# A two-layer linear-attention and gated-MLP kernel: new engine assignments, new order numbers, and a shorter assumed transfer time

## The chip, the cores and the metric

The kernel runs on one core of one Trainium2 chip. The core has engines with instruction queues of their own: TensorE (PE, matrix products), VectorE (DVE), ScalarE (ACT), GpSimd (POOL) and SyncE (SP, which here only starts transfers). Each queue is worked off in order; semaphores hold an instruction back until what it reads is ready. Transfers between HBM and on-chip memory run on 16 DMA engines and are started from SP's or ACT's queue.

The metric is the device time of one execution in microseconds (us). Before the change the median of three runs is 387.3 us (387.19, 387.30, 387.80).

## The reference

`x` is 2048 rows of 512 values, bf16. Two layers, with the same weights in both, each made of an attention block A and an MLP block B, both on a layernorm of `x` and added to it:

```
q, k, v = split(layernorm(x) @ wqkv)              # 32 heads of 16
pq, pk  = q @ w_phi[h], k @ w_phi[h]              # 16 x 16 per head
phi     = concat(softmax(p), softmax(-p))         # 32 features, for q and for k
kv, z   = phi_k^T @ v, sum over rows of phi_k
x      += ((phi_q @ kv) / (phi_q @ z + 1e-6)) @ wo

g, u    = layernorm(x) @ W_gate, layernorm(x) @ W_up     # 1376 columns
x      += (max(g, 0) * u) @ W_down
```

## The kernel before, in words

**Tiles and stages.** The 2048 rows are 16 tiles of 128 rows, grouped in five slabs of 2, 4, 4, 4 and 2 tiles (`SLABS`). A stage name has the layer and the slab: `a12` is the norm ahead of attention in layer 1 (the second), slab 2; `g12` the norm ahead of the MLP. For each slab: `layernorm` takes statistics on DVE (`bn` numbers), then applies mean and scale on DVE, ACT or POOL, then turns the tile, either on PE with an eviction out of PSUM or, for the 13 slabs in `XPOSE` and a few more, by a transposing transfer from SP (L916). `keys` makes k and v on PE, exponentials on ACT, their sums per head (`Zk`) on DVE, reciprocals on DVE or ACT (`rz`), the eviction of v on ACT or DVE (`vc`) and the product of v with the reciprocals (`vh`, two halves) on POOL or DVE; small products add up `kvsum`. When all slabs have been through `keys`, `sums` prepares the small matrices, and per slab `queries` and `attend` follow: exponentials of the queries, their sums, a reciprocal, and a factor per row and head, which is spread over the feature rows. For slabs 0 and 1 the spreading is done on PE (`spread`, scaling `em` on DVE straight out of PSUM, or after an eviction by ACT); for the others by two transfers through DRAM (`aTo`, `abT`) and scalings `es` on DVE or POOL. The sums of most slabs also go out to DRAM and back (`zao`, `zai`), after an eviction `za`. Then come the attention products, four evictions per slab (`ot`, on ACT or DVE), the product with `wo`, the next norm, and `glu`. Attention needs the sums over all rows, so the second layer's key work runs slab by slab beside the first layer's MLP, and its attention starts when the last slab has been through.

**The beginning.** Before the first key product can run, `fold` multiplies the key weight by `w_phi`, once, so that the features come straight out of one product: the four row blocks of the key weight (wk0 to wk3) are turned on PE (`wtr`, L732) and evicted (`ftk`), `w_phi` is laid out as a block-diagonal matrix (`BD`, one DVE product at L830 which reads the tile `wphi`), and four products give `Wkp`, evicted by `fck`. The query weight (wq0 to wq3) comes by transposing transfers and is folded later. The loads, in program order: x0 and x1 (one tile each), the four key blocks, wphi (16 KB in 32-byte pieces), x2 (two tiles), wv, x4, x8, x12 (four tiles each, x4 holds tiles 4 to 7), the query blocks, wo and the MLP weights. Eight warm-up products and 22 filler products on an array of ones keep PE busy while it waits.

**What sets the order.** Nothing in the program's text does. Every operation is recorded with its engine, a cost and what it reads and writes. `schedule` then goes through a simulated time and always takes the operation that can start earliest by its costs; between equals, the one with the lower number in the table `TURNS` (one number per operation, in hundredths of a microsecond). `plan` sorts each engine's operations by the simulated start and sets the semaphore waits. The table `ENG` says which engine gets an operation that could go to several: `'ld/...'` the queue of a load, `'ap/...'` a norm's application, `'ot/...'`, `'vc/...'`, `'vh/...'`, `'rz/...'`, `'es/...'`, `'em/...'`, `'za/...'` as above, `'ms/...'` a memset. A transfer is counted with a time for its bytes and latency, plus a `delay`: `LOADLATE` for the loads, `LATE` (in ns) for all transfers behind them (transposes, `aTo`, `abT`, `zao`, `zai` and the transposed MLP rest `hx`):

```
reads=[R("y", yb)], writes=R_yT(b, r0 + j), ..., issue=XISSUE, delay=XDELAY + LATE)      # L916
o.finish = max(qfree + 0.25 * self.DMA_LAT + o.lat, LAND.get(o.land, 0.0))
```

Neither the numbers nor `LATE` exist on the chip; they only decide how the instructions stand in the five queues.

Of the kernel before, what the change touches and what calls it, by code (L numbers as in the profile page):

```python
# [30 lines left out]
 'ap/a10/0': 'pool',  # L31
 'ap/a11/0': 'pool',
 'ap/a11/1': 'pool',
 'ap/a12/0': 'act',
# [8 lines left out]
 'ap/g01/3': 'act',  # L43
 'ap/g02/2': 'act',
 'ap/g03/3': 'act',
# [5 lines left out]
 'ap/g12/2': 'act',  # L51
 'ap/g12/3': 'act',
# [10 lines left out]
 'em/11/11': 'dve',  # L63
 'em/11/13': 'dve',
 'es/02/0': 'pool',
 'es/02/1': 'pool',
 'es/03/0': 'pool',
 'es/03/1': 'pool',
 'es/04/0': 'pool',
 'es/04/1': 'pool',  # L70
 'es/04/2': 'pool',
 'es/12/0': 'pool',
 'es/12/1': 'pool',
 'es/13/1': 'pool',
 'es/13/2': 'pool',
 'es/14/0': 'pool',
 'fck0': 'dve',
 'fck1': 'act',
 'fck3': 'act',
 'ftk1': 'act',  # L80
 'ld/x1': 'act',
# [3 lines left out]
 'ms/kvs eps 0': 'pool',  # L85
 'ot/00/0': 'dve',
 'ot/00/1': 'act',
 'ot/00/2': 'dve',
 'ot/01/3': 'dve',
 'ot/02/1': 'dve',  # L90
 'ot/02/2': 'dve',
 'ot/02/3': 'dve',
 'ot/03/2': 'dve',
 'ot/03/3': 'dve',
 'ot/04/0': 'dve',
 'ot/04/1': 'dve',
 'ot/04/2': 'dve',
 'ot/04/3': 'dve',
 'ot/10/1': 'act',
 'ot/10/2': 'dve',  # L100
 'ot/11/1': 'dve',
 'ot/12/0': 'dve',
 'ot/12/2': 'dve',
 'ot/13/0': 'dve',
 'ot/13/1': 'dve',
 'ot/13/2': 'dve',
 'ot/13/3': 'dve',
 'ot/14/1': 'dve',
 'ot/14/3': 'dve',
# [9 lines left out]
 'rz/1/0': 'act',  # L119
# [5 lines left out]
 'rz/1/15': 'act',  # L125
 'rz/1/3': 'act',
 'rz/1/4': 'act',
 'rz/1/5': 'act',
# [4 lines left out]
 'vc/0/7': 'dve',  # L133
 'vc/1/1': 'dve',
 'vc/1/13': 'dve',
 'vc/1/4': 'dve',
 'vc/1/5': 'dve',
 'vc/1/6': 'dve',
 'vc/1/7': 'dve',
 'vh/0/10/0': 'dve',  # L140
# [7 lines left out]
 'vh/0/6/1': 'dve',  # L148
 'vh/0/9/0': 'dve',
 'vh/0/9/1': 'dve',  # L150
 'vh/1/1/1': 'dve',
 'vh/1/11/0': 'dve',
 'vh/1/12/0': 'dve',
 'vh/1/13/1': 'dve',
 'vh/1/14/0': 'dve',
 'vh/1/14/1': 'dve',
 'vh/1/15/1': 'dve',
 'vh/1/3/0': 'dve',
 'vh/1/4/0': 'dve',
 'vh/1/5/1': 'dve',  # L160
 'vh/1/6/0': 'dve',
 'vh/1/6/1': 'dve',
 'vh/1/7/0': 'dve',
 'vh/1/8/1': 'dve',
 'vh/1/9/1': 'dve',
# [34 lines left out]
 'za/02': 'dve',  # L200
 'za/12': 'dve',
# [1210 lines left out]
```

## Time and profile before

| | us |
|---|---|
| median of three runs | 387.3 |
| the profiled execution | 386.95 |
| its span, first to last instruction | 385.2 |
| PE busy | 373.0 |
| DVE busy | 274.9 |
| ACT busy | 194.0 |
| POOL busy | 79.1 |

The profile is of one execution. A PE that is busy by this table is not PE at its peak, since products are pipelined; the time in which it is not busy (12.2 us) is idle time for certain. Most of the matrix products are recorded through one helper, so that one line, L728, stands for products of many stages; tiles and stretches of time tell them apart. Evictions out of PSUM have the lines L839 (DVE) and L842 (ACT). "Idle before" tells what ended an engine's wait.

### The profile page before, as it was taken

The numbers are of one execution on the slowest core, as the hardware profiler recorded it, in microseconds if no ns is written. First come the engines' busy times: TensorE is split into PE (matmuls) and PEld (weight loads), VectorE is DVE, ScalarE is ACT, GpSimd is POOL, SyncE is SP. The second block draws the span as 40 slices with busy tenths as digits, with TensorE's granted clock in tenths as the row PEclk, the third lists the DMA queues.
The fourth block names the chain that finished last, engine by engine and source line by source line (L and its number), as shares of the span: only waits on it lengthen the run. The fifth ranks groups of instructions, "written<-read, shape, count | busy, mean of one in ns | idle before, by whom it ended". The sixth has DMA issues, their size and how long they took to land.

```text
span 385.2 us, 8848 instructions
## 1 busy us (share of the span) xinstructions
PE 373.0 (97%) x3644; PEld 200.1 (52%) x3693; DVE 274.9 (71%) x559; ACT 194.0 (50%) x434; POOL 79.1 (21%) x68
## 2 busy tenths in 40 slices
PE   7999998999999999999999999989999999999996
PEld 4655454574445444454566455466544544445663
DVE  6999999878754795756299987678954666644333
ACT  4999999562430524255346579983262311413310
POOL 1087740030240521132023531004002110000000
PEclk9999999999999999999999999999999999999999
DMA  7997201142460222022002010214433121221011
GB/s 234 186 325 180 43 3 58 64 114 57 86 141 26 76 41 56 0 57 41 9 0 43 15 32 3 83 43 138 109 73 127 31 71 41 56 55 43 0 36 55
DMA packets 56969, 27.44 MB, mean 71 GB/s; under 512 B 39296, under 2 KB 55264, under 8 KB 56928
## 3 DMA queue, kind: packets, MB, share of 16 engines
q1 hardware_dynamic: 55824, 26.36, 27.6%
q10 hardware_dynamic: 1104, 0.51, 0.5%
q8 instruction: 29, 0.48, 0.5%
q14 instruction: 12, 0.10, 0.1%
HBM read 14.73 MB, written 4.00 MB: 49 GB/s over the span
## 4 chain that ended last, share of the span: by engine, by line
PE 77%; DVE 11%; ACT 5%; DMA 3%; issue 2%; SPq 2%; ACTq 0%
PE pb L728 72%; DVE stats L866 4%; PE pb L1001 2%; DMA wphi<-in_A_w_phi_dram 1%; DVE Zk L975 1%; ACT ytile L908 1%; DVE x_sb L1229 1%; SPq L916 1%; ACT expq L1070 1%; PE pb L1159 1%; DMA abT<-spread 1%; DMA yG<-ytile 1%; DVE ytile L911 1%; ACT gate_sb L1281 1%; SPq L1147 1%
## 5 line engine op out<-in xcount | busy, mean ns | idle before, releaser
L728 PE MATMUL pb<-yG,Wu 128*128 128x512 bf16 (+1 forms) x394 | 95.5, 336 | 1.1 <-DVE abT L839 0.3
L728 PE MATMUL pb<-Wd,hT 128*128 128x512 bf16 (+3 forms) x350 | 95.9, 372 | 0.5 <-issue 0.2
L728 PE MATMUL pb<-yG,Wg 128*128 128x512 bf16 (+1 forms) x394 | 93.3, 336 | 0.2
L1281 ACT ACTIVATE gate_sb<-pb 128x512 bf16<-128x512 f32 x80 | 46.9, 595 | 85.2 <-PE pb L728 63.9
L1283 DVE TENSOR_TENSOR hT<-gate_sb,pb 128x512 bf16<-128x512 bf16 x80 | 54.0, 682 | 49.7 <-PE pb L728 30.5
L1229 DVE TENSOR_TENSOR x_sb<-x_sb,pb 128x512 bf16<-128x512 bf16 x59 | 39.4, 679 | 26.2 <-PE pb L728 26.2
L728 PEld LDWEIGHTS pb<-yG,Wu 128*128 128x128 bf16 x400 | 38.9, 98 | 32.6 <-DVE abT L839 0.8
L728 PEld LDWEIGHTS pb<-yG,Wg 128*128 128x128 bf16 x400 | 38.8, 98 | 31.5 <-issue 0.6
L728 PEld LDWEIGHTS pb<-Wd,hT 128*128 128x128 bf16 (+1 forms) x363 | 34.8, 98 | 35.5 <-issue 1.1
L989 POOL TENSOR_TENSOR vhat<-vsb,rZk 128x544 bf16<-128x544 bf16 x29 | 31.9, 1118 | 79.7 <-ACT rZk L982 30.1
L1192 POOL TENSOR_TENSOR expq<-expq,abT 128x1024 bf16<-128x1024 bf16 (+1 forms) x12 | 21.5, 1799 | 123.5 <-DVE expq L1192 46.9
L866 DVE BATCH_NORM_STATS2 stats<-x_sb 128x6 f32<-128x512 bf16 x60 | 40.1, 683 | 0.3
L728 PE MATMUL pb<-wv,yA 128*128 128x512 bf16 x123 | 36.8, 379 | 0.5 <-issue 0.3
L728 PE MATMUL pb<-Wkp,yA 128*128 128x512 bf16 x123 | 35.7, 379 | 0.3 <-DVE yA L839 0.2
L1070 ACT ACTIVATE expq<-pb 128x512 bf16<-128x512 f32 x64 | 34.5, 621 | 1.2 <-PE pb L728 0.8
L728 PE MATMUL pb<-yA,Wqp 128*128 128x512 bf16 (+1 forms) x152 | 34.0, 335 | 1.1 <-issue 0.8
L728 PE MATMUL pb<-wo_sb,oT 128*128 128x512 bf16 x123 | 33.4, 379 | 0.2 <-ACT oT L842 0.2
L975 DVE TENSOR_REDUCE Zk<-expk 128x64 f32<-128x1024 bf16 x20 | 24.0, 1207 | 2.6 <-ACT expk L969 2.5
L969 ACT ACTIVATE expk<-pb 128x512 bf16<-128x512 f32 x40 | 22.0, 611 | 4.1 <-PE pb L728 3.0
L1249 ACT ACTIVATE gate_sb<-pb 128x192 bf16<-128x192 f32 x16 | 5.3, 329 | 33.7 <-PE pb L728 33.5
L908 ACT ACTIVATE ytile<-x_sb,nmr,rstd 128x512 bf16<-128x512 bf16 x27 | 20.8, 809 | 1.9 <-DVE nmr L900 1.8
L728 PEld LDWEIGHTS pb<-yA,Wqp 128*128 128x128 bf16 x160 | 14.3, 98 | 13.0 <-issue 1.3
(105 smaller groups left out, 395.8 us busy)
## 6 DMA issues: line engine op xcount, KB each, us to landing
abT<-spread SPq DMA_DIRECT2D x32, 128.0 KB
out_dram<-x_sb SPq DMA_DIRECT2D x15, 128.0 KB, 1.7
x_sb<-in_A_x_dram SPq DMA_DIRECT2D x3, 512.0 KB, 7.2
Wu<-in_B_W_up_dram SPq DMA_DIRECT2D x1, 1280.0 KB
Wg<-in_B_W_gate_dram SPq DMA_DIRECT2D x1, 1280.0 KB, 12.5
Wd<-in_B_W_down_dram SPq DMA_DIRECT2D x1, 1280.0 KB
sums_scr<-abT SPq DMA_DIRECT2D x5, 256.0 KB, 2.3
Zs<-sums_scr SPq DMA_DIRECT2D x5, 256.0 KB, 2.7
```

What stands on the lines that cost most here:

```text
L728: op("pe", lambda e: e.matmul(view(ps), lhsT, rhs, start=start, stop=stop), reads=reads, writes=[ps], occ=max(25.0, 0.4167 * n + 2.6), lat ...
L866: op("dve", lambda e: e.bn_stats(stats[:, t, :], src()), reads=[res], writes=[R("st", t)], occ=580, lat=680, name=f"bn{t}")
L908: op("act", (lambda t, yb: lambda e: e.activation(ytile[:, yb, :], x_sb[:, t, :], ACT.Identity, bias=nmr[:, t, :], scale=rstd[:, t, :]))(t ...
L969: op("act", (lambda i, s, pk: lambda e: e.activation(expk(i)[:, s, :], full(pk), ACT.Exp, scale=1.0 - 2.0 * s))(i, s, pk), reads=[pk], wri ...
L975: op("dve", (lambda i, zb: lambda e: e.tensor_reduce(Zk[:, zb, :], expk(i).rearrange("p s (h f) -> p (s h) f", f=16), AX.X, ALU.add))(i, z ...
L989: op(eng, (lambda i, s, vb, rz: lambda e: e.tensor_tensor(vhat(i)[:, s], vsb[:, vb, :, :], rZk[:, rz, s * 32:(s + 1) * 32].unsqueeze(2).to ...
L1001: ins = e.matmul(ps.f32()[32 * i:32 * i + 32, g * 34:g * 34 + 34], expk(tiles[j])[:, sg, f0:f0 + 32], vhat(tiles[j])[:, sg, 8 * c + 2 * i: ...
L1070: op("act", (lambda c0, s, ps: lambda e: e.activation(eqv(st)[:, c0:c0 + per, s, :], ps.f32()[:, 0:per * n].rearrange("p (c n) -> p c n", ...
L1192: op(eng, lambda e: e.tensor_tensor(part, part, abT[:, c].rearrange("p (s n) -> p s n", s=2)[:, :, 0:n], ALU.mult), reads=Re + [R("abT", c ...
L1229: op("dve", lambda e: e.tensor_tensor(x_sb[:, t, :], x_sb[:, t, :], full(ps), ALU.add), reads=[R("x", t), ps], writes=[R("x", t)], occ=597 ...
L1281: op("act", (lambda gb, pg, k: lambda e: e.activation(gate_sb[:, gb, 0:k], pg.f32()[:, 0:k], ACT.Relu))(gb, pg, k), reads=[pg], writes=[R( ...
L1283: op("dve", (lambda gb, hb, pu, k: lambda e: e.tensor_tensor(hT[:, hb, 0:k], gate_sb[:, gb, 0:k], pu.f32()[:, 0:k], ALU.mult))(gb, hb, pu, k),
```

## The change

Three things are replaced: entries of `ENG`, all of `TURNS` (3,256 numbers become 3,258, since some operations on another engine are recorded as two), and `LATE`. No function is changed.

Loads: `wphi` goes from ACT's queue to SP's, and the key blocks change queues: wk0 and wk2 on SP, wk1 and wk3 on ACT (before: wk0 and wk2 on ACT, wk1 and wk3 on SP). By the order numbers of the two tables the loads stand like this:

```
before  ACT: x1, wk0, wphi, wk2, (activation table)
        SP:  x0, wk3, wk1, x2, x4, wv, x8, wq0, Wl, wq3, wq1, Wd(rest), wq2, wo, x12, wo, Wu, Wg, ...
after   ACT: x1, wk1, (activation table), wk3
        SP:  x0, wphi, wk0, wk2, x2, x4, wv, x8, wq0, wq1, wq3, Wd(rest), x12, wq2, Wl, Wu, Wg, wo, ...
```

The array of ones keeps its 512 columns, and the value weight (wv) stays ahead of the query weight.

```
 ENG = {...
- 'ap/a10/0': 'pool',
+ 'ap/a10/0': 'act',
+ 'ap/a11/2': 'act',
+ 'ap/g02/0': 'act',
+ 'ap/g03/2': 'act',
- 'ap/g12/2': 'act',
- 'ap/g12/3': 'act',
- 'em/11/11': 'dve',
- 'es/02/1': 'pool',
- 'es/03/0': 'pool',
+ 'es/02/2': 'pool',
+ 'es/02/3': 'pool',
...
+ 'ftk0': 'dve',
+ 'ftk3': 'act',
+ 'ld/wk0': 'sp',
+ 'ld/wk1': 'act',
+ 'ld/wk2': 'sp',
+ 'ld/wk3': 'act',
+ 'ld/wphi': 'sp',
- 'ms/kvs eps 0': 'pool',
+ 'ms/kvs eps 1': 'pool',
+ 'ms/vsb ones': 'pool',
- 'ot/00/1': 'act',
- 'ot/00/2': 'dve',
+ 'ot/00/3': 'act',
...
+ 'ot/10/0': 'dve',
- 'ot/10/1': 'act',
- 'ot/10/2': 'dve',
...
- 'rz/1/0': 'act',
+ 'rz/1/2': 'act',
- 'rz/1/5': 'act',
+ 'vc/1/0': 'dve',
- 'vc/1/13': 'dve',
- 'vc/1/4': 'dve',
+ 'vc/1/11': 'dve',
+ 'vc/1/2': 'dve',
+ 'vc/1/3': 'dve',
+ 'vc/1/9': 'dve',
...
+ 'za/11': 'dve',
 TURNS = """
-0 50 126 150 63 100 0 315 189 257 378 1154 441 766 960 635 1217 ...
+0 126 50 189 230 63 0 378 252 315 441 960 504 635 1023 766 1763 ...
...
-ZALL=(...); ...; LATE=600
+ZALL=(...); ...; LATE=400
```

Without an entry, `ot` goes to ACT (in slab 0 its odd ones to DVE), `vc` to ACT, `vh` to POOL, `rz`, `es` and `za` to DVE, DVE and ACT, and `ftk` to ACT for even and DVE for odd blocks. Taken together, in the second layer's keys `vc` on DVE goes from 6 to 9 of 16, `vh` on DVE from 15 to 17 of 32 and `rz` on DVE from 5 to 6 of 16; the first layer's keys keep their counts.

More of the change, by code (lines that the diff above doesn't have):

```diff
@@ L62 @@
  'em/11/03': 'dve',
- 'em/11/11': 'dve',
  'em/11/13': 'dve',
  'es/02/0': 'pool',
- 'es/02/1': 'pool',
- 'es/03/0': 'pool',
+ 'es/02/2': 'pool',
+ 'es/02/3': 'pool',
  'es/03/1': 'pool',
  'es/04/0': 'pool',
- 'es/04/1': 'pool',
  'es/04/2': 'pool',
  'es/12/0': 'pool',
- 'es/12/1': 'pool',
- 'es/13/1': 'pool',
- 'es/13/2': 'pool',
+ 'es/12/2': 'pool',
+ 'es/13/0': 'pool',
  'es/14/0': 'pool',
+ 'es/14/1': 'pool',
  'fck0': 'dve',
@@ L84 @@
  'ms/kvs 0 1': 'pool',
- 'ms/kvs eps 0': 'pool',
+ 'ms/kvs eps 1': 'pool',
+ 'ms/vsb ones': 'pool',
  'ot/00/0': 'dve',
- 'ot/00/1': 'act',
- 'ot/00/2': 'dve',
+ 'ot/00/3': 'act',
  'ot/01/3': 'dve',
  'ot/02/1': 'dve',
- 'ot/02/2': 'dve',
- 'ot/02/3': 'dve',
+ 'ot/03/1': 'dve',
  'ot/03/2': 'dve',
  'ot/03/3': 'dve',
- 'ot/04/0': 'dve',
  'ot/04/1': 'dve',
- 'ot/04/2': 'dve',
- 'ot/04/3': 'dve',
- 'ot/10/1': 'act',
- 'ot/10/2': 'dve',
+ 'ot/10/0': 'dve',
  'ot/11/1': 'dve',
- 'ot/12/0': 'dve',
+ 'ot/11/2': 'dve',
+ 'ot/12/1': 'dve',
  'ot/12/2': 'dve',
+ 'ot/12/3': 'dve',
  'ot/13/0': 'dve',
@@ L106 @@
  'ot/13/2': 'dve',
- 'ot/13/3': 'dve',
- 'ot/14/1': 'dve',
- 'ot/14/3': 'dve',
+ 'ot/14/2': 'dve',
  'rz/0/1': 'act',
@@ L148 @@
  'vh/0/6/1': 'dve',
+ 'vh/0/8/0': 'dve',
  'vh/0/9/0': 'dve',
- 'vh/0/9/1': 'dve',
- 'vh/1/1/1': 'dve',
+ 'vh/1/0/0': 'dve',
+ 'vh/1/1/0': 'dve',
+ 'vh/1/10/1': 'dve',
  'vh/1/11/0': 'dve',
  'vh/1/12/0': 'dve',
- 'vh/1/13/1': 'dve',
+ 'vh/1/12/1': 'dve',
  'vh/1/14/0': 'dve',
  'vh/1/14/1': 'dve',
+ 'vh/1/15/0': 'dve',
  'vh/1/15/1': 'dve',
- 'vh/1/3/0': 'dve',
- 'vh/1/4/0': 'dve',
+ 'vh/1/3/1': 'dve',
+ 'vh/1/4/1': 'dve',
  'vh/1/5/1': 'dve',
  'vh/1/6/0': 'dve',
- 'vh/1/6/1': 'dve',
- 'vh/1/7/0': 'dve',
+ 'vh/1/7/1': 'dve',
  'vh/1/8/1': 'dve',
- 'vh/1/9/1': 'dve',
+ 'vh/1/9/0': 'dve',
  'xp/a02': 'pe',
@@ L344 @@
 XPOSE=("a02","a03","a04","a11","a12","a13","g01","g02","g03","g12","g13","g04","g14")
-ZALL=((0,2),(0,3),(0,4),(1,1),(1,2),(1,3),(1,4)); LASTCUT=((0,384),(384,512)); LOADLATE=(150,200); FILL=(14,8); PLAIN=('a01','a02'); LATE=600
+ZALL=((0,2),(0,3),(0,4),(1,1),(1,2),(1,3),(1,4)); LASTCUT=((0,384),(384,512)); LOADLATE=(150,200); FILL=(14,8); PLAIN=('a01','a02'); LATE=400
 ENGINES = ("sp", "act", "pe", "dve", "pool")
```

246 rows, old and new, of the table TURNS are left out of this document.

## The prediction

> **What bounds the kernel now.** I read the page first (busy shares, chain), then busy time by stretches, then the chain in order of time, and last the timeline and the DMA issues of the first microseconds.
>
> ```profile
> span 385.2 us, 8848 instructions
> ...
> PE 373.0 (97%) x3644; PEld 200.1 (52%) x3693; DVE 274.9 (71%) x559; ACT 194.0 (50%) x434; POOL 79.1 (21%) x68
> ...
> PE 77%; DVE 11%; ACT 5%; DMA 3%; issue 2%; SPq 2%; ACTq 0%
> ```
>
> PE is busy 97% of the span and carries 77% of the chain. No edit touches the number or shape of the matmuls, so 373.0 us of PE work stay; what can move is the 12.2 us in which PE is idle. Columns of the next rows: stretch, its length, busy us of PE, PEld, DVE, ACT and POOL with instruction counts, clock, DMA share, GB/s.
>
> ```profile
> 0.00:10.00 10.00, 7.97 (x56) 5.10 (x57) 6.29 (x22) 4.90 (x11) 1.73 (x11) 1.00 0.78 239
> 10.00:20.00 10.00, 9.73 (x74) 5.85 (x74) 10.00 (x24) 9.51 (x23) 0.21 (x1) 1.00 1.06 184
> 20.00:30.00 10.00, 9.65 (x129) 5.95 (x128) 10.00 (x24) 9.95 (x24) 9.39 (x9) 1.00 1.02 328
> ...
> 60.00:70.00 10.00, 9.10 (x179) 4.64 (x177) 9.70 (x23) 9.49 (x21) 0.00 (x0) 1.00 0.17 54
> ...
> 240.00:250.00 10.00, 9.82 (x119) 4.35 (x120) 6.31 (x16) 9.94 (x26) 0.00 (x0) 1.00 0.25 80
> 250.00:260.00 10.00, 9.02 (x141) 6.60 (x140) 7.63 (x19) 8.11 (x20) 0.00 (x0) 1.00 0.17 42
> ```
>
> The first 10 us leave PE idle for 2.03 us, and much of the 7.97 us is warm-up and filler matmuls on the array of ones. From 10 to 30 us DVE is full (10.00 of 10) and PE nearly so (9.73 and 9.65): a shift of the beginning finds no idle time there that would swallow it. 60 to 70 us has 0.90 us of PE idle time, 250 to 260 us 0.98, behind a stretch in which ACT is the full engine (9.94). So two places count: the first 10 us, and the hand-over into the second layer's attention.
>
> ```profile
> 1.72 5.55 DMA wphi<-in_A_w_phi_dram
> ...
> 9.56 2.38 DVE stats L866 x4
> ```
>
> Rows of the chain are start, length, what. The chain begins with the transfer of `wphi`; four statistics of DVE follow, of the row tiles 2 to 5. The timeline shows both queues and the wait (last bracket: idle time before, and what ended it):
>
> ```profile
> 0.79 0.40 SPq L751 DMA_DIRECT2D x_sb<-in_A_x_dram  x1
> ...
> 1.23 0.45 ACTq L761 DMA_DIRECT2D hT<-in_A_wqkv_dram  x1
> 1.25 0.88 SPq L761 DMA_DIRECT2D hT<-in_A_wqkv_dram  x2
> ...
> 1.72 0.46 ACTq L766 DMA_DIRECT2D wphi<-in_A_w_phi_dram  x1
> ...
> 2.18 0.94 SPq L751 DMA_DIRECT2D x_sb<-in_A_x_dram  x2
> 2.20 0.53 ACTq L761 DMA_DIRECT2D hT<-in_A_wqkv_dram  x1
> ...
> 2.76 1.28 ACT L789 ACT_TABLE_LOAD   x1 [2.76 <-issue]
> ...
> 3.17 0.51 SPq L769 DMA_DIRECT2D wv<-in_A_wqkv_dram  x1
> ...
> 4.70 0.30 DVE L891 BATCH_NORM_AGGREGATE mv<-stats 128x2 f32<-128x6 f32 x2
> ...
> 7.29 0.69 DVE L830 TENSOR_TENSOR hT<-wphi,mask 128x512 bf16<-128x512 bf16 x1 [2.29 <-DMA wphi<-in_A_w_phi_dram]
> ...
> 9.48 2.46 DVE L866 BATCH_NORM_STATS2 stats<-x_sb 128x6 f32<-128x512 bf16 x4
> ...
> 13.50 1.19 SPq L757 DMA_TRANSPOSE hT<-in_A_wqkv_dram  x1
> ...
> 16.10 0.44 SPq L751 DMA_DIRECT2D x_sb<-in_A_x_dram  x1
> ```
>
> ACT issues x1, wk0, wphi, wk2; SP issues x0, wk3 and wk1 (one row of two), x2 and x4 (one row of two), wv. DVE ends its last earlier work at 5.00 and stands 2.29 us until `wphi` lands. Landings, in us after the issue (last number, a median where the count is above 1):
>
> ```profile
> x_sb<-in_A_x_dram SPq DMA_DIRECT2D x1, 512.0 KB, 7.2
> hT<-in_A_wqkv_dram ACTq DMA_DIRECT2D x2, 128.0 KB, 5.9
> hT<-in_A_wqkv_dram SPq DMA_DIRECT2D x2, 128.0 KB, 3.7
> ...
> wphi<-in_A_w_phi_dram ACTq DMA_DIRECT2D x1, 16.0 KB, 5.5
> ```
>
> So x4, second of the row at 2.18 with 0.94 us for two issues, is issued at 2.65 and lands near 9.85. The slowest wk comes through ACT's ring, 5.9 us: issued 2.20, landed near 8.1.
>
> **The change part by part, and the sum.**
>
> *Loads.* `wphi` moves from ACT's third slot to SP's second: issue at 1.25 instead of 1.72, 0.47 us earlier. SP then issues wk0 and wk2 at its pitch of 0.44 us (0.88 for two), so near 1.7 and 2.1; x2 and x4, wv, x8 and the transposed query weights follow one slot later, 0.4 us each. ACT keeps x1, wk1 (1.23), the table load (1.28 us, now near 1.7) and wk3 behind it, near 3.0 instead of the 2.20 of today's fourth load. Gain, upper end: DVE cannot begin the `wphi` product before 5.00, which would be 2.29 us. But what is late next cuts that. The third statistic needs x4, and starts today at 9.48 plus two pitches of (2.46-0.68)/3 = 0.59, that is 10.67; x4 lands near 9.85 and has as many bytes ahead of it as before. So DVE wins at most 0.8 us. The new order numbers also put the statistic of tile 2 ahead of the first key-weight eviction, so a late x2 would hold that too. Lower end: x2 and x4 land 0.4 us later because of the extra slot, and nothing is won in front of them: 0.4 us lost. I take a gain of 0.45 us, nearest to the 0.47 of the issue rows, which needs no guess on how fast the transfer travels. No idle time follows to hide it, so it moves the end 1:1.
>
> The Trainium skill, page "DMA: Bandwidth & Descriptors", section "Issuing engines are not separate DMA queues", says that transfers started from SP, ACT or GpSimd run on the same 16 DMA engines and interleave, and that starting from several engines saves only the sequencer's issue time. By that rule no more than the issue time would be won and the result would be near 386.4; by the 0.8 us that the rows allow it would be 386.05. The trace agrees on the interleaving in so far as loads of both queues are under way together from 1.23 and 1.25 on.
>
> *Load order behind.* The array of ones keeps its 512-column memset and the value weight is behind x4 and ahead of the first query weight in both versions (order numbers 315 to 441 before, 378 to 504 after): nothing. x12 goes ahead of wq2. Today wq2 is issued at 13.50 and x12 at 16.10, and its first reader is numbered 2.4 us earlier than before, so the load gains the 2.6 us that its reader gains: 0, at worst one 0.68 us statistic of waiting. Small memsets change between POOL and DVE: one of them, 0.17 us at the start, where DVE waits anyway: 0.
>
> *Second-layer start.* Two evictions leave ACT for DVE in the stretch where ACT is full: one of the 256-column attention outputs of slab 0 (`ot/10`: two of four on DVE before, three after) and the sums of slab 1 (`za/11`).
>
> ```profile
> L839 DVE CAST vsb<-pb 128x512 bf16<-128x512 f32 x10 | 6.7, 682 | 0.1
> ...
> L839 DVE CAST oT<-pb 128x256 bf16<-128x256 f32 x11 | 4.2, 408 | 0.9 <-PE pb L1159 0.9
> ...
> L842 ACT ACTIVATE oT<-pb 128x256 bf16<-128x256 f32 x5 | 1.9, 445 | 4.2 <-PE pb L1159 4.2
> ...
> L842 ACT ACTIVATE abT<-pb 128x512 f32<-128x512 f32 x3 | 1.8, 591 | 4.4 <-POOL expq L1192 4.0 <-PE pb L1098 0.4
> ...
> L839 DVE COPY abT<-pb 128x512 f32<-128x512 f32 x2 | 1.4, 686 | 0.1
> ```
>
> ACT is relieved of 445+591 = 1036 ns; DVE, busy 6.31 of 10 there, takes 408+686. Upper end: the 0.98 us of PE idle time behind it. Lower end: a loss of 0.5, because in 250 to 260 us PE also waits on DVE, as this row has it:
>
> ```profile
> 252.25 0.40 PE L732 MATMUL pb<-ident,ytile 128*128 128x128 bf16 x4 [0.51 <-DVE ytile L911]
> ```
>
> I take 0.45 us gained, the row of the eviction that stands nearest to PE's next input, about the middle of 0 and 0.98.
>
> *Other assignments.* In the first layer's hand-over (60 to 70 us) two attention outputs go from DVE to ACT and one comes back; DVE (9.70) and ACT (9.49) are both full there, 0 with 0.4 us, one such eviction, to either side. In the second layer three more value evictions, two more value products and one reciprocal go to DVE, some norms and scalings change engine. PE runs on beside them (9.89 of 10 in the row below); taken at 0. Without that cover: DVE is full at 200 to 210 us, and the two value evictions of tiles 9 and 11 near it would cost 2 x 0.68 = 1.4 us.
>
> ```profile
> 200.00:210.00 10.00, 9.89 (x186) 6.68 (x186) 10.00 (x21) 5.17 (x11) 3.68 (x3) 1.00 0.20 28
> ```
>
> *LATE 600 to 400.* The constant adds no instruction. The planner believes that tiles brought by a transfer are ready 0.2 us sooner (0.4 where two transfers follow one another), so their readers stand earlier in the in-order queues. Cover today: PE's waits for transfers are short.
>
> ```profile
> PE pb L732 <- DMA hT<-in_A_wqkv_dram: 0.5, 1, 0.5
> ...
> PE pb L728 <- DMA yG<-ytile: 0.2, 1, 0.2
> ```
>
> ```profile
> DVE expq L1192 <- DMA abT<-spread: 2.7, 3, 1.4
> ```
>
> Taken at 0. Ends: a gain only where PE stands idle today for an input that has landed, which is in the 0.98 us already counted; a loss as in the third rival.
>
> Sum against the profiled execution, 386.95 us (span 385.2 and 1.75 around it): 386.95 - 0.45 - 0.45 = 386.05. That execution is 0.35 us under the median of 387.3, so the median after is 386.4. 0.2% (0.77 us) is about what a measurement can tell here from no change.
>
> **The rivals.**
>
> *No gain.* The weights and x tiles are the same bytes through the same DMA engines; the last key weight still lands near 8.1 and x2 holds DVE, and ACT's relief only moves the wait to DVE. For it: x2 and x4 stand one slot later. Against: the 2.29 us of DVE idle time names `wphi` alone. Both gains fall away: 386.95 + 0.35 = 387.3.
>
> *Slower by the ring.* SP's ring now has `wphi` ahead of wk0, wk2, x2 and x4. Its 16 KB take 5.5 us against 3.7 us for 128 KB on SP; if everything behind it in the ring is late by that difference of 1.8 us and by the slot of 0.4, x4 lands near 9.85 + 2.2 = 12.05, against 10.67 when DVE reads it today: DVE loses 1.4 us where 0.45 was taken as won, 386.4 + 0.45 + 1.4 = 388.25. The point from which it decides is an x4 that lands after 10.67. Against: ACT's ring has no small pieces any more and holds just two key weights, so what SP's ring loses, the other gives back. The same page of the Trainium skill, section "Queues, rings and completion order", says that on each DMA engine the descriptors of one ring are consumed in ring order, which is this rival's mechanism; no row here shows the order inside a ring.
>
> *Slower by earlier readers.* The transposes of `yG` take a median of 2.5 us over the run, and 3.2 between 80 and 120 us, where other transfers are around (first row: whole run; second: that stretch):
>
> ```profile
> yG<-ytile SPq DMA_TRANSPOSE x28, 2.5
> ```
>
> ```profile
> yG<-ytile SPq DMA_TRANSPOSE x8, 3.2
> ```
>
> There they are 0.7 us longer. The planner's margin shrinks by 0.2 us for each of the 13 slabs that `XPOSE` sends through the transposing transfer; if ten of them stop PE for 0.2 us, 2.0 us are lost: 386.4 + 2.0 = 388.4. It decides once PE's waits for transfers exceed 0.9 us beyond today's 0.7.
>
> *Larger gain.* `wphi` no longer waits behind wk0 and lands near 5: 0.8 us at the start in place of 0.45, and 0.98 in place of 0.45 in the second layer: 386.4 - 0.35 - 0.53 = 385.5.
>
> **How the numbers follow.** Forecast 386.4: 0.42 (own range 385.9 to 387.0, of which 0.30 faster by over 0.2%, 0.12 within). No gain, 387.3: 0.24. Ring: 0.12. Earlier readers: 0.13. Larger gain: 0.09. Faster 0.30 + 0.09 = 0.39; same 0.12 + 0.24 = 0.36; slower 0.12 + 0.13 = 0.25. Range 385.4 to 388.3: under it half of the larger gain, over it half of each slower case.
>
> **What would show it.** Right: DVE's `wphi` product starts before 6.9 and its four statistics before 9.2; the idle time of PE in 250 to 260 us below 0.7; ACT below 9.5 in 240 to 250 us. Wrong: DVE still starts the statistics at 9.4 or later, waiting for x2 or for a key weight; PE waits for transfers of transposed tiles over 1 us in total; DVE full beyond 220 us with PE waiting behind it.

## The result and the profile after

The kernel after takes 385.55 us (median of 8 executions, 384.78 to 386.95), beside 387.2 for the kernel before on the same chips: a ratio of 0.9959, 95% interval 0.9942 to 0.9975. That is 1.6 us faster (1.0 to 2.2). The forecast was 386.4 with a range of 385.4 to 388.3. The profiled execution took 385.75 us, 1.2 less than that of before.

The page of the kernel after, its first lines and the chain of work that ended last:

```profile
span 384.0 us, 8891 instructions
...
PE 376.7 (98%) x3693; PEld 200.7 (52%) x3693; DVE 279.3 (73%) x563; ACT 193.8 (50%) x435; POOL 73.3 (19%) x65
...
PE 95%; ACT 2%; DVE 1%; DMA 1%; issue 0%; ACTq 0%
```

PE is on 95% of the chain, where it was on 77%. A part of that is no gain: the page before shows 3644 products and 3693 weight loads, the page after 3693 of both. 49 records are missing before, and each leaves a hole that looks like idle time. So the 12.2 us of idle PE before, on which the prediction was built (and which the section on the profile before calls certain), were too many; after, with all records there, it is 384.0 - 376.7 = 7.3 us.

Busy time by stretches after, in the columns of the prediction's table (length; busy us of PE, weight loads, DVE, ACT, POOL; clock, DMA share, GB/s):

```profile
0.00:10.00 10.00, 8.21 (x60) 5.28 (x61) 7.38 (x23) 5.61 (x13) 2.16 (x12) 1.00 0.77 234
...
240.00:250.00 10.00, 10.00 (x127) 4.48 (x124) 7.48 (x18) 9.18 (x23) 0.00 (x0) 1.00 0.29 81
250.00:260.00 10.00, 9.20 (x136) 7.05 (x136) 8.11 (x18) 7.79 (x19) 0.00 (x0) 1.00 0.16 41
290.00:300.00 10.00, 10.00 (x53) 4.93 (x52) 6.62 (x11) 2.78 (x6) 2.12 (x1) 1.00 0.36 118
```

The loads, the start of DVE's work and the last evictions of the folded key weight (`Wkp`), from the timeline of the kernel after, and the same last row of the kernel before:

```profile
1.24 0.42 SPq L772 DMA_DIRECT2D wphi<-in_A_w_phi_dram  x1
...
1.72 1.28 ACT L795 ACT_TABLE_LOAD   x1 [1.72 <-PEq L1403]
1.75 0.49 ACTq L767 DMA_DIRECT2D hT<-in_A_wqkv_dram  x1
...
2.72 0.94 SPq L757 DMA_DIRECT2D x_sb<-in_A_x_dram  x2
...
5.07 0.66 DVE L836 TENSOR_TENSOR hT<-wphi,mask 128x512 bf16<-128x512 bf16 x1
...
7.52 0.69 DVE L872 BATCH_NORM_STATS2 stats<-x_sb 128x6 f32<-128x512 bf16 x1
...
9.16 1.87 DVE L872 BATCH_NORM_STATS2 stats<-x_sb 128x6 f32<-128x512 bf16 x3
9.42 1.61 ACT L848 ACTIVATE Wkp<-pb 128x512 bf16<-128x512 f32 x3
```

```profile
10.37 1.60 ACT L842 ACTIVATE Wkp<-pb 128x512 bf16<-128x512 f32 x3
```

`wphi` is issued at 1.24 and DVE makes its product at 5.07 with no wait before it (7.29 before). The three evictions of `Wkp` on ACT end at 9.42 + 1.61 = 11.03, where before they end at 11.97: the folded weight is there 0.94 us earlier. ACT's second key block is issued at 1.75, while the table load runs from 1.72 to 3.00: the load of the tables held no issue back.

The landings of the first loads after (last number: us from issue to landing), and two of PE's longest waits:

```profile
x_sb<-in_A_x_dram SPq DMA_DIRECT2D x1, 512.0 KB, 5.8
...
wphi<-in_A_w_phi_dram SPq DMA_DIRECT2D x1, 16.0 KB, 3.0
```

```profile
PE pb L813 <- DVE yG L798: 1.6, 1, 1.6
...
PE pb L1213 <- DVE yG L845: 0.6, 1, 0.6
```

`wphi` took 3.0 us where it took 5.5. x4, issued at 3.2, landed 5.8 later, at 9.0. No wait of PE for a transfer is left in the list.

### The profile page after: what moved, and what is told of

It is laid out like the page before. It is cut to its first block, busy times and chain, and to the rows that moved or that the text cites. A ratio compares the mean times of both kernels' runs of the same rounds, so it can differ in the third digit from the quotient of the medians.

```text
span 384.0 us, 8891 instructions
## 1 busy us (share of the span) xinstructions
PE 376.7 (98%) x3693; PEld 200.7 (52%) x3693; DVE 279.3 (73%) x563; ACT 193.8 (50%) x435; POOL 73.3 (19%) x65
## 4 chain that ended last, share of the span: by engine, by line
PE 95%; ACT 2%; DVE 1%; DMA 1%; issue 0%; ACTq 0%
PE pb L734 88%; PE pb L1007 3%; PE pb L1165 1%; PE pb L738 1%; ACT expq L1076 1%; DMA hT<-in_A_wqkv_dram 1%; PE pb L818 1%; PE pb L1104 1%; PE pb L1091 1%; PE pb L1213 0%; DVE expq L1231 0%; ACT abT L848 0%; PE pb L813 0%; DVE x_sb L1305 0%; DVE zm L1134 0%
## 5 line engine op out<-in xcount | busy, mean ns | idle before, releaser
L734 PE MATMUL pb<-yG,Wu 128*128 128x512 bf16 (+1 forms) x400 | 92.9, 336 | 0.0
L734 PE MATMUL pb<-yG,Wg 128*128 128x512 bf16 (+1 forms) x400 | 91.0, 336 | 0.0
L1198 POOL TENSOR_TENSOR expq<-expq,abT 128x1024 bf16<-128x1024 bf16 (+1 forms) x11 | 19.3, 1769 | 140.2 <-DMA abT<-spread 80.9
L995 POOL TENSOR_TENSOR vhat<-vsb,rZk 128x544 bf16<-128x544 bf16 x26 | 28.6, 1122 | 55.8 <-ACT rZk L988 24.8
L734 PE MATMUL pb<-Wkp,yA 128*128 128x512 bf16 x128 | 38.8, 379 | 0.3 <-issue 0.3
L734 PE MATMUL pb<-wv,yA 128*128 128x512 bf16 x128 | 38.8, 379 | 0.0
L734 PE MATMUL pb<-yA,Wqp 128*128 128x512 bf16 (+1 forms) x160 | 37.3, 338 | 0.0
L1076 ACT ACTIVATE expq<-pb 128x512 bf16<-128x512 f32 x64 | 35.6, 628 | 2.9 <-PE pb L734 2.6
L734 PE MATMUL pb<-wo_sb,oT 128*128 128x512 bf16 x128 | 35.3, 379 | 0.0
L914 ACT ACTIVATE ytile<-x_sb,nmr,rstd 128x512 bf16<-128x512 bf16 x29 | 22.5, 813 | 2.9 <-DVE nmr L906 2.8
```

The lines of the kernel that those rows point to most:

```text
L734: op("pe", lambda e: e.matmul(view(ps), lhsT, rhs, start=start, stop=stop), reads=reads, writes=[ps], occ=max(25.0, 0.4167 * n + 2.6), lat ...
L914: op("act", (lambda t, yb: lambda e: e.activation(ytile[:, yb, :], x_sb[:, t, :], ACT.Identity, bias=nmr[:, t, :], scale=rstd[:, t, :]))(t ...
L995: op(eng, (lambda i, s, vb, rz: lambda e: e.tensor_tensor(vhat(i)[:, s], vsb[:, vb, :, :], rZk[:, rz, s * 32:(s + 1) * 32].unsqueeze(2).to ...
L1076: op("act", (lambda c0, s, ps: lambda e: e.activation(eqv(st)[:, c0:c0 + per, s, :], ps.f32()[:, 0:per * n].rearrange("p (c n) -> p c n", ...
L1198: op(eng, lambda e: e.tensor_tensor(part, part, abT[:, c].rearrange("p (s n) -> p s n", s=2)[:, :, 0:n], ALU.mult), reads=Re + [R("abT", c ...
```

## The experiments

Each was timed beside the kernel before, so ratios are compared (0.001 is 0.39 us), with their 95% intervals. "Last key-weight eviction" is the end of the `Wkp` rows, as above.

**The loads alone, and all but the loads.** Two kernels, one the mirror of the other; the queue and place of every load is set by hand and all else stays:

```
 # in the kernel before:
+for o, (eng, at) in zip(prog.ops, LOADS_OF_AFTER):  o.eng, o.start = eng, at
 # in the kernel after:
+for o, (eng, at) in zip(prog.ops, LOADS_OF_BEFORE): o.eng, o.start = eng, at
```

> The kernel before, with the queues and issue order of the loads of the kernel after, and nothing else: no assignment, no order number and no LATE changes. The theory of the prediction (loads 0.45, hand-over 0.45): 386.75 us where before is 387.2, a ratio of 0.9988, and the last key-weight eviction ends 0.45 earlier than before's 11.97. Rival A, the loads' whole gain of 0.94 us (as the trace of after has it at 12 us) is carried to the end: 386.25, 0.9976. Rival B, the loads' gain is swallowed on the way (after is only 0.18 us ahead at 238 us) and the second layer's new order carries the 1.65: 387.0, 0.9995, with about 0.9 gained at 12 us and 0.2 at 238 us.

> The kernel after, with the queues and issue order of the loads of before; the rest of the change stays. The prediction: 0.45 is lost again, 386.0 where after is 385.55, a ratio of 0.9970 to before. Rival A (the loads carry 0.94): 386.5, 0.9982. Rival B (the loads are swallowed on the way): 385.75, 0.9963. That the new order was made for the new landings and is worse than the old one with the old landings would give above 387.2.

The loads alone: 387.95 us, ratio 1.0013 (0.9993 to 1.0033), no gain. The rest without the loads: 388.35, 1.0023 (1.0007 to 1.0039), slower than before. Together they win 0.41%. Neither half is worth anything alone, so a sum of separate terms cannot give the result; the halves fit each other. The timelines say how. First PE in the kernel before (two rows: eight products that turn the first two key blocks, and what follows them), then the same eight with the loads alone.

```profile
4.89 1.06 PE L732 MATMUL pb<-ident,hT 128*128 128x128 bf16 x8
5.75 1.27 PE L812 MATMUL pb<-yG 128*128 128x256 bf16 x5
```

```profile
6.33 0.61 PE L734 MATMUL pb<-ident,hT 128*128 128x128 bf16 x8 [1.56 <-DMA hT<-in_A_wqkv_dram]
```

PE's queue is in order. Before, it turns wk3 and wk0 first, each the first block of its queue, and starts at 4.89. With the new loads wk0 stands behind `wphi` and wk3 behind wk1; PE stands 1.56 us and starts at 6.33. DVE had no wait for `wphi`, but the last key-weight eviction ended only at 11.45. That is 0.52 us earlier than before, and nothing of it shows in the median. The profiled execution took 386.6, near the low end of its times (386.27 to 390.31); where the others gave the gain back stays open.

With the loads undone (PE, DVE and ACT):

```profile
6.36 0.58 PE L740 MATMUL pb<-ident,hT 128*128 128x128 bf16 x4 [1.98 <-DMA hT<-in_A_wqkv_dram]
...
7.62 0.69 DVE L838 TENSOR_TENSOR hT<-wphi,mask 128x512 bf16<-128x512 bf16 x1 [2.84 <-DMA wphi<-in_A_w_phi_dram]
...
11.77 1.57 ACT L850 ACTIVATE Wkp<-pb 128x512 bf16<-128x512 f32 x3
```

Here PE asks first for wk1, which now stands behind wk3 on SP's queue, and stands 1.98 us; DVE stands 2.84 us for `wphi`, and the eviction ends at 13.34, 2.3 us later than after. No idle time behind swallowed that: the span is 2.0 us longer at the end.

**`wphi` alone, in the kernel before.** It goes on SP's queue third, behind wk3; the key blocks stay where PE wants them.

```
-ACT: x1, wk0, wphi, wk2, (table)      SP: x0, wk3, wk1, x2, x4, wv, ...
+ACT: x1, wk0, wk2, (table)            SP: x0, wk3, wphi, wk1, x2, x4, wv, ...
```

> The kernel before, with one edit: wphi leaves ACT's queue and goes on SP's, third, behind wk3 (wk1, x2, x4, wv, x8, wq0 one slot later each); the key blocks stay on their queues and PE reads them in before's order. wphi is issued at about 1.7, no earlier than before's 1.72. The rule that another queue saves no more than issue time: no change, 387.35, a ratio of 1.000, and the last key block lands near 8. The theory of queue relief (the trace of after): wk2 is issued at 1.75 instead of 2.20 and lands near 6.3 instead of 8.1, wphi takes 3 us instead of 5.5 and lands near 4.8, the last key-weight eviction ends 0.9 earlier than 11.97, and the end comes 0.9 earlier: 386.45, 0.9977. The rival that the gain is lost on the way, as in the loads alone: 387.35 with a landing near 6.3.

386.16 us, 0.9987 (0.9977 to 0.9997): 0.5 us faster (0.1 to 0.9). The timeline and the landings:

```profile
1.23 0.94 ACTq L763 DMA_DIRECT2D hT<-in_A_wqkv_dram  x2
...
1.71 0.43 SPq L768 DMA_DIRECT2D wphi<-in_A_w_phi_dram  x1
...
5.05 0.69 DVE L832 TENSOR_TENSOR hT<-wphi,mask 128x512 bf16<-128x512 bf16 x1
...
9.67 1.60 ACT L844 ACTIVATE Wkp<-pb 128x512 bf16<-128x512 f32 x3
```

```profile
hT<-in_A_wqkv_dram ACTq DMA_DIRECT2D x2, 128.0 KB, 3.6
...
wphi<-in_A_w_phi_dram SPq DMA_DIRECT2D x1, 16.0 KB, 3.3
```

`wphi` is issued at 1.71, as before (1.72), and yet DVE's product starts at 5.05 and the last eviction ends at 11.27, 0.7 earlier. So what was won is not issue time of `wphi`. It is time to landing: 3.3 us instead of 5.5 for `wphi`, and 3.6 instead of 5.9 for ACT's second key block, wk2, which no longer stands behind `wphi` (the first block's landing is in neither trace). The issue of wk2 moves up too, from 2.20 to 1.72, second of ACT's row at 1.23; but wk2 lands near 5.3 instead of 8.1, far more than this half microsecond. How the gain divides between `wphi` and wk2 was not tried. The Trainium skill, page "DMA: Bandwidth & Descriptors", section "Issuing engines are not separate DMA queues", says that starting transfers on several engines saves only the issue time. This kernel's rows disagree: the queue also changed the time to landing.

**`wphi` back on ACT, in the kernel after.** The key blocks take the free places in the order in which PE of the kernel after reads them; x12 and all behind it stays early.

```
-ACT: x1, wk1, (table), wk3            SP: x0, wphi, wk0, wk2, x2, ...
+ACT: x1, wk0, wphi, wk3, (table)      SP: x0, wk1, wk2, x2, ...
```

> The kernel after, with wphi back on ACT's third place and the four key blocks on the free places in the order in which PE reads them; x12 and all that follows stays early, as in after. The prediction's term for wphi: 0.45 lost, 386.0, a ratio of 0.9970. The trace's 0.94 at 12 us lost again: 386.5, 0.9983. Theory that the kernel with the loads undone lost by x12 and by the blocks' order alone, and that wphi's queue is worth little: 385.6, 0.996, with the last key-weight eviction near 11.1.

385.94 us, 0.9969 (0.9951 to 0.9987): 0.4 us above after. The two intervals overlap, so by time alone this could be nothing; the timeline (DVE, PE, ACT) shows the place of it:

```profile
7.33 0.69 DVE L838 TENSOR_TENSOR hT<-wphi,mask 128x512 bf16<-128x512 bf16 x1 [2.48 <-DMA wphi<-in_A_w_phi_dram]
...
8.07 0.34 PE L736 MATMUL pb<-hT 128*128 128x128 bf16 x3 [1.56 <-DVE hT L838]
...
10.13 1.60 ACT L850 ACTIVATE Wkp<-pb 128x512 bf16<-128x512 f32 x3
```

DVE waits 2.48 us for `wphi` again, PE 1.56 us for DVE's product, and the last eviction ends at 11.73, 0.70 later than after. The span ends 0.6 later. From both sides, then, the queue of `wphi` is worth about 0.4 to 0.5 us in the times, of which only the 0.5 is clear of noise, and 0.6 to 0.7 in the traces.

**All loads undone, but the blocks fitted.** As the last one, but the loads behind wq0 also go back to the places of before (x12 behind wq2 and a part of wo).

```
-SP: ... wq0, wq1, wq3, Wd(rest), x12, wq2, Wl, Wu, Wg, wo ...
+SP: ... wq0, Wl, wq3, wq1, Wd(rest), wq2, wo, x12, wo, Wu, Wg ...
```

> The kernel after, with the loads of before (wphi on ACT's third slot), but with the four key blocks put on them in the order in which PE of the kernel after reads them: wk1 on SP's and wk0 on ACT's first place, wk2 SP's second, wk3 ACT's last. The theory that PE's order and the landings have to fit: of the 2.8 us by which the undone loads were slower than after, 1.4 come back, the last key-weight eviction ends near 11.97 instead of 13.34 and the time is 386.5 (385.55 + 0.94), a ratio of 0.9978; what is then still won against before, 0.85, is the new order's. The rival that wphi alone made the undone loads slow: 388.3, 1.0023. The rival that the whole gain of the change is at the start: 387.3, 1.000.

387.56 us, 1.0028 (1.0010 to 1.0046). That is the time of the rival by which `wphi` alone made the undone loads slow (1.0023), but not for its reason, as the timeline shows. It follows (ACT, SP, DVE, PE), and behind it that of the kernel after for the same reader (third of the row at 16.05) with two PE rows that are used below, and before's reader:

```profile
9.52 1.60 ACT L850 ACTIVATE Wkp<-pb 128x512 bf16<-128x512 f32 x3
...
14.53 0.44 SPq L759 DMA_DIRECT2D x_sb<-in_A_x_dram  x1
...
19.48 0.69 DVE L874 BATCH_NORM_STATS2 stats<-x_sb 128x6 f32<-128x512 bf16 x1 [2.02 <-DMA x_sb<-in_A_x_dram]
...
20.82 0.39 PE L736 MATMUL pb<-wv,yA 128*128 128x512 bf16 x1 [1.71 <-DVE vsb L847]
```

```profile
8.69 0.61 PE L734 MATMUL pb<-hT 128*128 128x128 bf16 x8
...
9.13 0.71 PE L818 MATMUL pb<-yG 128*128 128x256 bf16 x5
...
11.46 0.42 SPq L757 DMA_DIRECT2D x_sb<-in_A_x_dram  x1
...
16.05 1.88 DVE L872 BATCH_NORM_STATS2 stats<-x_sb 128x6 f32<-128x512 bf16 x3
```

```profile
20.72 0.70 DVE L866 BATCH_NORM_STATS2 stats<-x_sb 128x6 f32<-128x512 bf16 x1
```

The start is not late (9.52 + 1.60 = 11.12, after: 11.03). The loss comes at 19.48: x12 is issued at 14.53 instead of 11.46, DVE stands 2.02 us for it, and PE 1.71 us for the value eviction behind. In the kernel after the same statistic runs at 16.05 + 2 x 0.6 = 17.25, in the kernel before at 20.72, with x12 issued at 16.10. From the issue to the reader that waits it is 4.95 us here and 4.53 in the next kernel; by these two, an estimate, x12 came at 16.0 to 16.4 after, 0.8 us or more ahead of its reader, and at 20.6 or later before, when its reader starts at once. The reader moved 3.5 us ahead, and the load with it. The wait for x12 is the only one for a transfer that this kernel's lists of waits have from 10 to 60 us. Against the kernel with `wphi` back, which differs in these later loads, the step is 0.0059, 2.3 us, with about 1.0 to either side (an estimate from the two intervals); the spans of the two profiled executions differ by 1.1 us.

**x12 alone**, two places later in the kernel after:

```
-SP: ... Wd(rest), x12, wq2, Wl, Wu, ...
+SP: ... Wd(rest), wq2, Wl, x12, Wu, ...
```

> The kernel after, with the transfer of x12 put behind wq2 and a slice of the last columns on SP's queue, three places later; everything else as after. In the kernel with the loads undone and the blocks fitted, DVE stood 2.02 us for x12 and PE 1.71 us behind it. Theory that the readers of x12 have moved ahead and need the early transfer: x12 lands 1.6 to 3 us later than 15.89, its statistic (17.24 in after) waits, and with a margin of 1.35 us before it 0.3 to 1.7 us are lost: 386.0 to 387.2, a ratio of 0.997 to 1.000. The prediction, which took the order of x12 and wq2 at 0: 385.55, 0.9959.

385.97 us, 0.9969 (0.9953 to 0.9985): 0.4 us above after, at the lower end of what was expected, with intervals that overlap.

```profile
12.91 0.51 SPq L759 DMA_DIRECT2D x_sb<-in_A_x_dram  x1
...
17.44 0.69 DVE L874 BATCH_NORM_STATS2 stats<-x_sb 128x6 f32<-128x512 bf16 x1 [0.62 <-DMA x_sb<-in_A_x_dram]
```

1.45 us later in the issue became 0.62 us of waiting on DVE. Its key weights were done 0.46 us earlier than after's (10.57), its end is 0.3 us later. The kernel with the blocks fitted lost more, but there x12 was issued 1.6 us later still and other loads had moved too; the two were not told apart.

**The gap in front of PE filled.** In the kernel with the loads undone, the sixth product on the array of ones is made five times:

```
+def five(e, fn=prog.ops[42].fn):   # prog.ops[42]: the sixth warm-up product
+    for _ in range(4): fn(e)
+    return fn(e)
+prog.ops[42].fn = five
```

> The kernel with the loads undone, and four more 512-column products on the ones between the sixth and the first key block, in the 2 us in which PE stood there (4.39 to 6.36). No work that the result needs is added or moved. Theory of the clock (PE takes 0.83 ns a column until it has been busy without a break for some 3 us, then 0.43; the break at 4.39 put the change off to 10.3): the change comes before 8, the last key-weight eviction ends near 12.3 instead of 13.34, the time is 387.3 instead of 388.35. Rival, the landings alone set the start: 388.35, ratio 1.0023, the eviction at 13.3.

```profile
10.80 1.61 ACT L850 ACTIVATE Wkp<-pb 128x512 bf16<-128x512 f32 x3
...
19.51 0.69 DVE L874 BATCH_NORM_STATS2 stats<-x_sb 128x6 f32<-128x512 bf16 x1 [0.85 <-DMA x_sb<-in_A_x_dram]
```

The last eviction ended at 12.41, as expected (12.3, where it was 13.34). The time did not follow: 387.96 us, 1.0036 (1.0022 to 1.0050). The last row says why: x12, as late as before, holds DVE at 19.51. The three kernels with the late x12 finish their first weights at 11.12, 12.41 and 13.34, and their first addition to `kvsum` that follows (27.84 in the kernel after) ends at 30.09, 30.12 and 30.24. The kernel with the loads undone had two bounds, the late start and the late x12, which end within 0.15 us of each other; an earlier start is worth nothing while the next load sets the pace.

**The second-layer hand-over undone.** In the kernel after, the two evictions go back to ACT:

```
 ENG = {...
-'ot/10/0': 'dve',
+'ot/10/1': 'act', 'ot/10/2': 'dve',
-'za/11': 'dve',
```

> The kernel after, with the evictions ot/10/0, ot/10/1, ot/10/2 and za/11 on the engines of before, so that ACT has the two evictions back in the second layer's hand-over; loads, LATE and all other assignments as after. The prediction (the relief of ACT is what gains there): 0.45 is lost, 386.0, a ratio of 0.9970, and ACT is above 9.5 of 10 in 240 to 250 us again. Rival B (the gain of about 1.0 us between 238 and 262 us comes from the new order and the other assignments): 385.6, 0.9960, with the same stage times at 262 us as after. All of the 1.0 us by these four: 386.55, 0.9983.

385.18 us, 0.9939 (0.9925 to 0.9954). Nothing is lost. The stretches:

```profile
240.00:250.00 10.00, 10.00 (x133) 4.60 (x134) 6.72 (x16) 9.69 (x25) 0.00 (x0) 1.00 0.29 81
250.00:260.00 10.00, 9.09 (x135) 6.93 (x128) 8.09 (x17) 7.69 (x19) 0.00 (x0) 1.00 0.15 41
```

ACT is at 9.69 again (9.18 after), as foretold; PE in 250 to 260 us is busy 9.09 instead of 9.20. The relief of ACT is real, but PE's idle time there differs by just 0.11 us in these traces, and the time shows no loss. PE's waits there are for DVE either way: the row of 0.6 us at L1213 stands in this kernel's list as in after's, and the one for `ytile` is 0.36 us here and 0.25 after. Its row here:

```profile
PE pb L738 <- DVE ytile L917: 0.4, 1, 0.4
```

**Slab 3's scaling undone.** `es/13` as before (first part on DVE, second and third on POOL):

```
-'es/13/0': 'pool',
+'es/13/1': 'pool', 'es/13/2': 'pool',
```

> The kernel after, with the scaling of slab 3 of the second layer (es/13) on the engines of before: its first part on DVE instead of POOL, the second and third on POOL. In the order of before DVE stands 1.8 us there for a transfer of the reciprocals and PE 0.7 us behind it, near 295 us; in after PE is never idle there. Theory that this assignment is what won it: PE waits 0.5 to 0.9 us near 295 us again and the time is 386.2, a ratio of 0.9976. The prediction (other assignments 0): 385.55, 0.9959, and the wait was the order's.

The expectation came from this place in the order of before (the kernel with the loads alone, all records there): DVE, then PE, and the stretches of time.

```profile
294.92 0.69 DVE L1194 TENSOR_TENSOR expq<-expq,abT 128x1024 bf16<-128x1024 bf16 x1 [1.77 <-DMA abT<-spread]
...
296.13 0.82 PE L730 MATMUL pb<-yG,Wu 128*128 128x512 bf16 x3 [0.68 <-DVE abT L841]
```

```profile
250.00:260.00 10.00, 9.02 (x128) 6.74 (x129) 7.67 (x16) 7.78 (x18) 0.00 (x0) 1.00 0.18 42
290.00:300.00 10.00, 9.32 (x44) 4.03 (x42) 4.39 (x7) 2.97 (x5) 4.20 (x2) 1.00 0.42 131
```

DVE stands 1.77 us in its queue for a transfer of the reciprocals, with an eviction behind it that PE needs. The kernel with `es/13` undone: 385.11 us, 0.9940 (0.9922 to 0.9958), and no such wait:

```profile
290.00:300.00 10.00, 10.00 (x53) 4.87 (x51) 5.00 (x9) 2.72 (x5) 3.53 (x2) 1.00 0.38 121
```

PE is busy 10.00 of 10, as in the kernel after. So the assignment is not what won it. What is left is the place of the reader in the new order, which was not undone alone.

**LATE back at 600**, with the order numbers of after; some 30 instructions change places.

```
-LATE=400
+LATE=600
```

> The kernel after with LATE = 600 in place of 400, all assignments and order numbers as after; some 30 of the instructions change places in their queues. The prediction (LATE costs and gains nothing): 385.55, a ratio of 0.9959, with no wait of PE for a transfer in either. The theory that earlier readers stop PE: faster than after, 385.0 or below. The theory that the smaller margin is itself a gain (readers stood behind work that could wait): 386.2 or more.

385.67 us, 0.9962 (0.9941 to 0.9983), after's own ratio: the constant neither costs nor gains.

**Three fillers cut**, 256 columns to 32, in the kernel after:

```
+for i in (45, 46, 47):   # fillers ahead of wk0 and wk2
+    prog.ops[i].fn = product on ones[:, 0:32]
```

> The kernel after, with three of the 256-column filler products (at 5.76, 5.97 and 6.61 us, ahead of key blocks that have landed) cut to 32 columns. In after's trace PE is never idle from 4.53 on and these three take 0.64 us at the half rate: if PE is the bound there, the last key-weight eviction ends 0.3 to 0.4 earlier than 11.03 and the time is 385.15, a ratio of 0.9949. Rival, the landings (wk2 at 6.47) and DVE's queue set it: 385.55, 0.9959. Rival, less work on PE puts off its change to the full rate: 385.9 or more.

385.12 us, 0.9959 (0.9945 to 0.9974), the same ratio as after. The profiled execution, at 386.52 the longest of six, shows what PE's rate does:

```profile
7.66 0.63 PE L738 MATMUL pb<-ident,hT 128*128 128x128 bf16 x4
...
8.09 0.63 PE L738 MATMUL pb<-ident,ytile 128*128 128x128 bf16 x4
```

At 7.66 four products of 128 columns take until 8.09, 0.107 us each; in the kernel after, eight take from 8.69 to 9.13, 0.055 each, and that rate is there from 7.4 on. Here it came at 8.7, and the last key-weight eviction ended at 11.64. The last section comes back to this.

**Together**: `wphi` third on SP with the blocks fitted, the cut fillers, and `ot/10` and `za/11` as before.

> The kernel after, with what the runs so far showed no loss from: wphi third on SP (behind wk0) and the blocks where PE's order wants them, the three filler products cut to 32 columns, and ot/10 and za/11 on the engines of before. If the gains add (0.3 at the start by a first pair of blocks that lands near 4.3, 0.4 by the fillers, 0.2 by the evictions): 384.7, a ratio of 0.9936. If PE and the landings already share the bound of the start, no more than after: 385.5, 0.9957. If the cut fillers put off PE's full rate: 386 or more.

385.26 us, 0.9947 (0.9930 to 0.9964). Its last key-weight eviction ends at 10.17, 0.86 earlier than after, and its span is 0.5 us shorter. The interval holds both of the first two expectations. By time it is not told apart from after, nor are the kernels with the hand-over or `es/13` undone; all of them beat the kernel before.

## Why the prediction was right, and where it was not

The time lies in the range and on the side that had the highest chance. The 0.9 us forecast is just short of the interval's lower end of 1.0. The time is that of the *larger gain* (385.5), but not by its parts. That the sum came out this near is in part luck: one of its two terms gave nothing that can be measured, and the new order, put at 0, gave more than either.

*Loads, 0.45.* Right in size for the move of `wphi`: 0.5 us (0.1 to 0.9) by moving it alone in the kernel before, 0.4 by moving it back in the kernel after, which by itself could be noise. The reason given for the number was wrong. It was taken from the 0.47 us of issue time, and the kernel in which `wphi` was issued no earlier won as much; what counted was the time to landing (3.3 instead of 5.5) and the key block behind `wphi` on ACT's queue (landed near 5.3 instead of 8.1). Three details failed: x4 was not late next (landed at 9.0, read at 9.16 + 0.6 = 9.8); ACT's second block did not wait for the table load (1.75, not 3.0); and the last block's landing stood beside `wphi` as a bound before (8.1 against 7.26, with PE waiting 0.5 us for it), which the prediction had only in a rival. The observations named for it came as stated: the product at 5.07 (before 6.9), the statistics at 7.52 and 9.16 (before 9.2).

*Load order behind, 0.* The step that failed most. It holds only because reader and load moved together, as the text said; what it missed is what hangs on it. With the readers ahead and the later loads on the places of before, about 2.3 us are lost (1.3 to 3.3, an estimate), not "one 0.68 us statistic"; the wait that the trace shows for it is DVE's 2.02 us for x12. In the same way the key blocks' queues were taken as free, and the loads without the new order of PE won nothing.

*Second-layer start, 0.45.* Wrong. ACT fell below 9.5 as foretold (9.18), but PE's idle time in 250 to 260 us stayed at 0.80 where under 0.7 was asked for, and undoing the two evictions costs no time that can be measured (0.9939 against 0.9959; by the two intervals at most 0.1 us, an estimate). The step that failed is the path. PE's waits there are for DVE in every order: 0.51, 0.28 and 0.18 us in the order of before (the loads alone), 0.56 and 0.36 with the two evictions back on ACT, 0.56 and 0.25 in the kernel after (the 0.56 is the row of 0.6 in the list of waits, at 252.5 us). ACT was full, but PE did not wait for it, as the prediction's own row of 0.51 us had shown; nor did its relief move a wait to DVE, as the rival *no gain* had it, since the wait stood there before.

*Other assignments, 0.* Those that were put back alone are nothing, as said. But the rest of the change, the kernel with `wphi` back on ACT, is 0.9969 against the kernel before, 1.2 us (0.5 to 1.9): the new order, together with the loads that fit it, carries most of the result. Between 10 and 380 us PE is idle 2.96 us in the kernel with the loads alone, which has the order of before and all records, 2.18 in the kernel with `wphi` back and 2.22 in the kernel after. With the key weights done 0.24 us ahead of before (11.73 against 11.97), the traces so show about 1.0 of the 1.2 us. In the kernel after, the 0.68 at 295 us and 0.39 at 30 to 40 us went away and 0.98 became 0.80; 0.31 at 220 to 230 and 0.24 at 40 to 50 came new. Which entry did it isn't settled: `LATE`, the four evictions and `es/13`, each put back alone, lose nothing.

*LATE, 0.* Right, by the run with 600.

*The rivals.* The ring: x4 landed at 9.0, before 10.67, though `wphi` and two key blocks were ahead of it. Earlier readers: PE's list has no wait for a transfer left; the reader that stood too early was one in the order of before, DVE's at 295 us. No gain: 1.0 us or more was won, and the last key block did not stay near 8.1; wk2, now on SP's queue, landed near 6.4 (issued near 2.2, 4.2 us to landing).

*Idle time.* 12.2 us were counted; the kernel with the loads alone, in the same order and with all records, has 384.8 - 375.4 = 9.4, though PE starts its key blocks later there. 2.03 and 0.98 were real (the latter stands at 0.98 in the kernel with the loads alone), but in the quiet stretches the holes are missing records. 80 to 90 us, before and with the loads alone, in the same order:

```profile
80.00:90.00 10.00, 9.70 (x97) 6.22 (x97) 6.51 (x15) 5.59 (x11) 2.13 (x1) 1.00 0.45 88
```

```profile
80.00:90.00 10.00, 10.00 (x99) 6.38 (x97) 6.25 (x14) 5.35 (x11) 2.12 (x1) 1.00 0.50 98
```

0.30 us of idle time before, none with all records.

## What to carry to other kernels

When a change moves a load and the instruction that reads it, the two have one price: undo one of them, and what is measured is their mismatch, here about 2.3 us against a gain of 1.6 for the whole change. So, for each moved load, find the first reader on each in-order queue, its place before and after, and the margin between landing and reading. Before a full engine is relieved, see which engine the waits behind it name. And compare the number of products with that of weight loads before idle time is read from a page.

## What the runs showed of the hardware

*A small transfer's time depends on the queue that starts it.* `wphi`, 16 KB in 32-byte pieces, took 4.5, 5.5, 5.6, 5.9 and 5.9 us in the five kernels that start it from ACT, and 2.7 to 4.0 us in the nine that start it from SP, issued between 1.24 and 1.72 in all. On ACT's queue it stood third in all five; third on SP's queue, behind x0 and one key block, it took 3.3 and 3.5 us. Why was not tried.

*PE runs at half its rate at first, and the moment at which that ends differs between traces with the same start.* In the kernel after, eight products of 128 columns take from 8.69 to 9.13 (0.055 us each); in the kernel before, eight take from 4.89 to 5.75 (0.107 each). The clock column of the profile says 1.00 in both. The full rate came at 5.0, 5.5, 7.3, 7.3 and 7.4 us in five kernels with the same start as after (x12 later, the hand-over undone, LATE 600, `es/13` undone, after itself), whose key weights were done at 10.57, 10.81, 10.96, 11.23 and 11.03. It came at 10.3 where PE had stood still from 4.4 to 6.4, and at 6.0 with that gap filled. The Trainium skill, page "TensorE: Matmul & The Clock Gate", section "What's actually happening", has a window of about 3.4 us that must pass busy and whose phase is not tied to the kernel's start. These runs agree: PE works from 1.64 us on in the five kernels, with no gap above 0.5 us, and the full rate comes 3.4 to 5.8 us later, between one such window and two. So half a microsecond at the start of a single trace can be chance. This is argued from the five kernels, since no kernel was traced twice, and it bears on every difference of that size between two traces here.
